# Coefficients of a state-space kernel multiplied untransposed and summed by fp32 matmuls, the table of one half built 256 channels wide, five last stores, and a new order of work

## The chip, the cores and the metric

The program runs on one core of a Trainium2 chip. The metric is the device time of one execution in microseconds, the median of several runs. A profiled execution gives a trace besides: every instruction of every engine with its start and length. TensorE (PE) does matmuls and reads its stationary operand with weight loads (PEld); VectorE (DVE), ScalarE (ACT) and GpSimd (POOL) work on tiles in on-chip memory (SBUF) and on the accumulators (PSUM); SyncE (SP) issues transfers.

## What is computed

Two branches over the same x of 2048 tokens by 512 channels are mixed by a gate per token. Branch a is a diagonal complex state-space model, applied as a causal convolution of each channel with a kernel K of 2048 taps; branch b adds a gated feed-forward result to the two tokens with the largest router value and passes the rest through.

```python
x = A_u
g = _sigmoid((x * gate_w).sum(-1, keepdims=True))
# branch a
dt = jnp.exp(log_dt)[:, None]
A = A_re + 1j * A_im
Bc = B_re + 1j * B_im
Cc = C_re + 1j * C_im
logdA = dt * A
dB = dt * Bc
P = jnp.exp(logdA[:, :, None] * l[None, None, :])
K = jnp.einsum("dn,dnl,dn->dl", Cc, P, dB).real
# y = causal convolution of u with K along the tokens, plus u * Dskip
# branch b
r = x @ w_r
idx = jnp.argsort(-r, axis=-1)[:, :C]      # C = 2
# y = (silu(x_sel @ w_gate) * (x_sel @ w_up)) @ w_down * sigmoid(r_sel), added to those two rows of x
return g * a + (1 - g) * b
```

The product C·B·dt (complex, 512 channels by 128 states) is what this text calls the coefficients. K at a tap is the sum over the states of coefficient times a power of the decay.

## The kernel before

**An order written out.** The program is a list of 651 operations, each with the buffers that it reads and writes. `ORDER` gives, as numbers in base 36, one sequence of all operations; each engine runs its own operations in that sequence, and `SECOND` says for an operation that two engines can run (an eviction by ACT or DVE, say) which of them does. Waits follow from the buffers alone: an operation waits for the last of what it needs, and for everything that used its memory before, since many buffers share places (`PLACES` gives the PSUM banks). An engine that waits holds up all that stands behind it in its own order. The operations were listed and their order was found ahead of time, with a planned cost for each.

**Stages.** (1) The parameters are loaded (`prm_l`, six tiles of 128 x 512 and log_dt), dt = exp(log_dt) is taken on ACT (`DTP`, line 589), and `DG` (line 590, DVE) holds four diagonal matrices of dt. Short matmuls with `DG` both transpose the parameters and scale them (`scaled`, line 593): the decay's real part (`AL`), its angle (`tb_`), and the two parts of B (`bd`). (2) Eight groups of transposes turn x (line 811), evicted to `XT`; reversed halves are folded (`fold`, `pm`). (3) 32 groups of four 128x512 matmuls (`forward`, line 938) transform x; their evictions fill `X`. (4) Beside that DVE and ACT build tables for each half of the channels (256 each): powers of the decay at 64 coarse taps (`tab1`, the `TP` tiles) and at fine taps (`tab2`, the `EB` and `DI` tiles, and from them, with the coefficients, the `R` tiles). (5) `kgen` multiplies the two tables on PE (line 957), which gives K at the taps needed; `kspec` transforms K (line 1009). (6) `products` multiplies the spectra on DVE (lines 1032 to 1063), `inverse` transforms back (line 1098), and each 128-token tile is scaled and stored. Routing and the feed-forward of the two tokens (lines 802 to 916) run between.

**What the change touches.** The coefficients: `ptr` (line 606) transposes C on PE into PSUM (`cc`), `scaled` transposes and scales B (`bd`), an eviction copies `cc` to SBUF (`CS`, line 633), two DVE products of 128x1024 make the four partial products (`CM1`, `CM2`, lines 634 and 635), and `WT` (lines 617 to 624, four DVE instructions of 128x256 in fp32, with a permuting read) sums them into `WW`. In `tab2` (lines 764 to 784) a loop of two passes builds the `R` tiles of a half, 128 channels each: products with `WW` (lines 772 and 773, 1024 elements), a difference and a sum (lines 774 and 775, 512 elements each), a negated copy `nb`, four products of 1792 elements (line 783) and two of 768 (line 784). `kgen` reads the tiles of pass 0 in its first eight steps and those of pass 1 in the rest (line 948). The first table load of ACT is not in the program text; it stands ahead of the first Exp. The parameter tile A_re is issued on ACT's queue, as are C_im and B_im. `warm` (line 642) are filler matmuls on PE, ten groups. The last output stores (line 1125) are eight of one tile of 128 tokens by 256 channels, four on SP and four on ACT.

Of the kernel before, what the change touches and what calls it, by code (L numbers as in the profile page):

```python
# [355 lines left out]
def small_mats():  # L356
# [15 lines left out]
    "00500200600300000101g00800400701l00u01k00900a00k00y00z01p01j01200e00d01601000b00h01300q01701801101400f00n02200c01501b02106r01m01o01d02l01z01x01c06u02f"  # L372
    "02j02n01w01v02m01y01r00j02t06s01f02h00o00i01t02g01e02u02o02k01q02r02v02i03301u02s02p02w03402a02002802306t02q02y00g02c01h00l09l03503602902705u02x02b019"
    "03705v03804l05o02605i03i09k03906v05w03j03k00w01a03l05j03a03m05k05p06w06x03n03o05s00p04m00t03p04n0b405q01n03q06y03r0b30250b205r07703z03s03t03b02d0b505m"
    "04204o03u07805t00r00m03v00v0b604r04p01i04q02z03w0790b704303x05l04004s03005n0b804100x06107a04704u04t06004v04403206205y04w04x04d05x03103c07b0b904y03f05f"
    "02404a0700720510bj04z07107c05006z05z05g04c07304b0740bi07504805206l07d04906m0530bl04e0bd07604504f05h03y07f0bb04g0540670580bk05507e07p06n0bm07h0bo056046"
    "06605907g05706904h05a0bc04i06a0ba07k0bn04j06807i06c07m07n01s07o06d0640be06b07q07j05b05c07r02e06p0bf06o05d04k07s06e05e0630bg06q00s06i07v06506j06g06f08w"
    "07t09m07l08106k09n08007y08308x0840bh08209q09o08508607z09p08707u07w07x08908a0bp08808v08b08y0bq09r06h03d0bs0br09t08d08c0bv09u08g09v08m09s08f08e08i08j09w"
    "09x08k08l0by0c00a008h08n09y0bw0a10c108o08p08q0bu08r0a20a308s09a0bt0c20c30c50a70a409z08t0bz09b08u08z0a809c09d0bx0a90aa0a509h0920ab0c40900c909e0930a609f"
    "0940c70ac0ca09i0910ad09g0950ce0cc0cb0c60al09j0cf0ci0cd0ch0c80cl0am0ck0cg0960cj0970cn0co0cm0cr0cq0cs03g0cp0cu0ct0cv0cx0an0cw0cy0d80dc0da03h0ap0980990d1"  # L380
# [19 lines left out]
def bass_gated_mix__ssm_conv_s4__moe_arch_mod__prompt_kernel(nc, A_u, A_A_re, A_A_im, A_B_re, A_B_im, A_C_re, A_C_im, A_log_dt, A_Dskip,  # L400
# [24 lines left out]
    with ExitStack() as es:  # L425
# [50 lines left out]
        def DMA(pairs, rd, wr, nbytes, eng=SP, **k):  # L476
            return P.op(eng, lambda h: [h.dma_start(o, i) for o, i in pairs], rd, wr, cost=0.5 * len(pairs), n=len(pairs), nbytes=nbytes, dma=True, **k)  # L477
# [724 lines left out]
```

## Time and profile before

| | us |
|---|---|
| median of 3 runs (lowest, highest) | 147.41 (147.23, 147.58) |
| the profiled execution | 148.09 |
| its span, first to last instruction | 146.3 |
| PE busy, DVE busy, ACT busy | 138.1, 137.3, 125.0 |
| granted PE clock | 1.000 |
| first matmul of the forward transform starts | 19.04 |
| last DVE instruction ends | 144.05 |
| issue of the last store ends | 144.42 |

Busy time is the union of an engine's instructions; consecutive instructions of DVE and ACT overlap by a little under 0.1 us, so that sums of lengths are larger than the time they take in a row. The profiled execution has 1.8 us outside its span. Where the prediction quotes a view, its columns are named there.

### The profile page before, as it was taken

To read this page: it belongs to the slowest core of one execution; us is meant where nothing else is said; L and a number is where in the kernel's file an instruction comes from. 1 tells how busy PE (TensorE), PEld (TensorE's weight loads), DVE (VectorE), ACT (ScalarE), POOL (GpSimd) and SP (SyncE) were. 2 spreads that over 40 slices of the span, in tenths; PEclk is the share of its full clock that TensorE was granted. 3 is DMA by queue.
4 is the path that set the end of the run, shared out by engine and by line. 5 is a ranking of instruction groups with operands and counts; after the bars stand their busy time and mean duration, and the time that the engine had idled before them with its cause. 6 is when DMAs were issued, how large, how long until landed. Compare 5 with 4: busy or idle time off the path is not lost.

```text
span 146.3 us, 3922 instructions
## 1 busy us (share of the span) xinstructions
PE 138.1 (94%) x1669; PEld 101.9 (70%) x1669; DVE 137.3 (94%) x195; ACT 125.0 (85%) x197; POOL 3.2 (2%) x14
## 2 busy tenths in 40 slices
PE   7967999999999999999989999989999999999992
PEld 2746855664666444697857779978774877888881
DVE  0699999999999999998999999999999999999993
ACT  4299999999999999999999897894999999796810
POOL 5001000000000000000000000100000000000000
PEclk9999999999999999999999999999999999999999
DMA  3999989401790000198000000449940001103165
GB/s 116 293 354 411 481 326 338 158 2 1 243 532 25 0 1 1 40 351 328 7 4 0 0 4 0 141 101 394 372 154 0 0 2 40 38 0 104 55 185 166
DMA packets 13610, 21.10 MB, mean 144 GB/s; under 512 B 2147, under 2 KB 9208, under 8 KB 13432
## 3 DMA queue, kind: packets, MB, share of 16 engines
q1 hardware_dynamic: 12584, 20.19, 39.3%
q10 hardware_dynamic: 1008, 0.66, 1.4%
q8 instruction: 13, 0.21, 0.6%
q14 instruction: 5, 0.04, 0.1%
HBM read 18.74 MB, written 4.20 MB: 157 GB/s over the span
## 4 chain that ended last, share of the span: by engine, by line
PE 49%; DVE 44%; ACT 2%; issue 2%; ACTq 1%; DVEq 0%
DVE AR L455 39%; PE ps L1098 17%; PE ps L938 14%; PE ps L957 3%; PE ps L1045 2%; PE ps L599 2%; DVE AR L462 2%; PE ps L647 1%; DVE AR L622 1%; PE ps L700 1%; PE ps L825 1%; PE ps L905 1%; PE ps L795 1%; ACTq L477 1%; PE ps L711 1%
## 5 line engine op out<-in xcount | busy, mean ns | idle before, releaser
L455 DVE TENSOR_TENSOR AR<-AR 128x1024 bf16<-128x1024 bf16 (+6 forms) x130 | 113.5, 933 | 3.6 <-ACT AR L466 2.8
L470 ACT ACTIVATE AR<-ps 128x1024 bf16<-128x1024 f32 (+7 forms) x63 | 51.1, 851 | 5.5 <-PE ps L1009 3.0
L466 ACT ACTIVATE AR<-ps 128x1024 bf16<-128x1024 int16 (+2 forms) x34 | 28.3, 891 | 3.6 <-PE ps L599 2.7
L938 PE MATMUL ps<-AR 128*128 128x512 bf16 x128 | 30.0, 379 | 0.0
L1098 PE MATMUL ps<-AR 128*128 128x256 bf16 x256 | 29.0, 273 | 0.0
L1098 PEld LDWEIGHTS ps<-AR 128*128 128x128 bf16 x256 | 24.9, 98 | 3.3
L938 PEld LDWEIGHTS ps<-AR 128*128 128x128 bf16 x128 | 12.1, 98 | 12.9
L1009 PE MATMUL ps<-AR 128*128 128x256 bf16 x160 | 19.1, 273 | 0.0
L957 PEld LDWEIGHTS ps<-AR 128*128 128x128 bf16 x512 | 18.1, 96 | 0.9
L957 PE MATMUL ps<-AR 128*128 128x84 bf16 (+1 forms) x512 | 18.4, 196 | 0.0
L1009 PEld LDWEIGHTS ps<-AR 128*128 128x128 bf16 x160 | 15.5, 98 | 3.1
L474 ACT ACTIVATE AR<-AR 128x256 int32<-128x256 f32 (+3 forms) x26 | 15.2, 612 | 0.1
L1107 ACT ACTIVATE AR<-ps,AR 128x256 bf16<-128x256 f32 x24 | 9.7, 479 | 2.3 <-PE ps L1098 2.2
L466 ACT ACTIVATE ps<-AR 128x256 f32<-128x256 bf16 x26 | 11.3, 488 | 0.1
L466 ACT ACTIVATE AR<-AR 128x1024 bf16<-128x1024 int16 (+4 forms) x12 | 9.4, 780 | 0.1
L647 PE MATMUL ps<-AR 128*128 128x464 bf16 x22 | 6.9, 444 | 2.0 <-DVE AR L470 1.0
L455 DVE TENSOR_TENSOR AR<-AR,ps 128x2048 bf16<-128x2048 bf16 (+1 forms) x6 | 7.1, 1210 | 0.2 <-PE ps L599 0.2
L706 PE MATMUL ps<-AR 128*128 128x512 f16 x24 | 6.2, 378 | 0.0
L1045 PE MATMUL ps<-AR 128*128 128x512 bf16 x24 | 5.8, 379 | 0.2 <-DVE AR L455 0.2
L809 PE MATMUL ps<-AR 128*128 128x128 bf16 x64 | 4.2, 219 | 1.3 <-DVE AR L455 1.3
L647 PEld LDWEIGHTS ps<-AR 128*128 128x128 bf16 x22 | 2.2, 113 | 4.2 <-issue 1.4
L809 PEld LDWEIGHTS ps<-AR 128*128 128x128 bf16 x64 | 3.7, 98 | 1.9 <-DVE AR L455 1.5
(74 smaller groups left out, 95.9 us busy)
## 6 DMA issues: line engine op xcount, KB each, us to landing
AR<-c_ksp SPq DMA_DIRECT2D x5, 512.0 KB, 7.1
AR<-in_A_u_dram SPq DMA_DIRECT2D x8, 256.0 KB, 5.3
AR<-out_dram SPq DMA_DIRECT2D x4, 512.0 KB, 9.4
AR<-c_inv SPq DMA_DIRECT2D x1, 2048.0 KB, 8.6
AR<-in_B_w_gate_dram SPq DMA_DIRECT2D x1, 1792.0 KB, 11.3
AR<-in_B_w_up_dram SPq DMA_DIRECT2D x1, 1792.0 KB, 16.8
out_dram<-AR SPq DMA_DIRECT2D x12, 128.0 KB, 2.2
AR<-c_fwd SPq DMA_DIRECT2D x4, 256.0 KB, 5.7
```

Of the source, the lines that this page charges most:

```text
L455: return P.op(DVE, lambda h: h.tensor_tensor(out=o, in0=a, in1=b, op=op), rd, wr, cost=tt_cost(o, a, b), **k)
L466: return P.op(ACT, lambda h: h.activation(out=o, in_=a, func=func, scale=scale, bias=bias), rd, wr, cost=0.185 + nel(o) * 0.833e-3 + (0.09 ...
L470: return P.op((ACT, DVE), (lambda h: h.activation(out=o, in_=a, func=ACTF.Copy), lambda h: h.tensor_copy(o, a)), rd, wr, cost=(0.185 + n * ...
L474: return P.op((ACT, DVE), (lambda h: h.activation(out=o, in_=a, func=ACTF.Copy, scale=c), lambda h: h.tensor_scalar(out=o, in0=a, scalar1= ...
L647: r = h.matmul(pb(0, 128, 0, (1, 464)), MSB(0, 128, 0, (0, 128)), MSB(0, 128, 0, (0, 464)), start=True, stop=True)
L809: last = h.transpose(bb(0, 128, db * 256 + t_ * 128, (1, 128)), U(0, 128, (2 * q + t_) * D + db * 128, (1, 128)), RV(0, 128, 0, (1, 128)) ...
L938: last = h.matmul(pb(0, 128, j * 512, (1, 512)), F[ft](0, 128, (kt * 2 + 1 - j) * 128, (1, 128)), pm[q](0, 128, kt * 512, (1, 512)), start ...
L957: last = hh.matmul(pb(0, 128, g // k * 512 + g % k * W4 + o, (1, n)), TP[h][1 - i // 2](0, 128, (b0 + g) * 128, (1, 128)), r[i](0, 128, (b ...
L1009: last = hh.matmul(pb(0, 128, n * 256, (1, 256)), KP[u](0, 128, tau * 128, (1, 128)), KC[h](0, 128, jg * 256, (1, 256)), start=(k == 0 and ...
L1045: r = hh.matmul(pb(0, 128, pm * 512, (1, W)), CB(0, 128, 128 * (k if part == 0 else 0), (1, 128)), b(0, 128, ((0, 3), (1, 2))[part][k] * 2 ...
L1098: r = hh.matmul(pb(0, 128, c0, (1, 256)), G(0, 128, ((par * 2 + part) * 4 + ft) * 512 + (2 * t2 + e) * 128, (1, 128)), X(0, 128, h * 8192 ...
L1107: return [hh.activation(out=U(0, 128, tb * D + h * HC, (1, HC)), in_=pb(0, 128, tb // 2 % 2 * 256, (1, HC)), func=ACTF.Copy, scale=SG(0, 1 ...
```

## The change

The list has 640 operations instead of 651. Its parts:

- **Coefficients.** `ptr`, the two matmul groups for B, the copy `CS`, the two products from PSUM and `WT` are gone. DVE multiplies C and B as they lie (channels not yet turned): `CM1` in one product of 1024 elements with an fp32 result, `CM2` in two of 512 (one of them negating). ACT makes an fp32 copy of dt (`DTF`) and four fp32 diagonal matrices (`DGS`) from an fp32 identity that POOL makes (`IDF`). `wsum`, two groups of eight fp32 matmuls, transposes, scales and adds in PSUM; one eviction rounds both parts into `WW` (on DVE), and `WN` is a negated copy of one part (on DVE).
- **Table.** Half 0 is built in one pass of 256 channels (`WIDE`), so `kgen(0)` reads one set of `R` tiles in all its steps; `EB`, `DI`, `NB`, `QA`, `QW` of that half move to other places. In both halves the difference and the sum become one instruction.
- **Small operations.** `LIN` lets DVE or ACT run eight operations of the routing and the gate; five of these and one copy go to ACT.
- **Stores.** The last eight stores become five: three of two tiles and two of one tile, of which only the last in the list is on ACT.
- **Head.** ACT's first instruction is an explicit table load; A_re goes to SP's queue.
- **Order.** `ORDER`, `SECOND` and `PLACES` are new throughout. Among much else: nine of the ten filler groups run ahead of the last transposes of x, the first copy of x to the output moves behind the down-projection's loads, three evictions of transposes and some scalings, negations and seeds change engine.

```diff
     def run(self, e, h):
         last = None
+        if e == ACT:
+            h.preload_act_table_set("exp_and_others")
+            last = 0
...
+WIDE = (0,)
...
+        def LIN(o, a, m, c, rd, wr):
+            one = isinstance(m, float) and m == 1.0
+            d = (lambda h: h.tensor_scalar(out=o, in0=a, scalar1=c, scalar2=None, op0=ALU.add)) if one else (lambda h: h.tensor_scalar(out=o, in0=a, scalar1=m, scalar2=c, op0=ALU.mult, op1=ALU.add)) if c is not None else (lambda h: h.tensor_scalar(out=o, in0=a, scalar1=m, scalar2=None, op0=ALU.mult))
+            f = ACTF.Copy if c is None or isinstance(c, float) else ACTF.Identity
+            P.op((DVE, ACT), (d, lambda h: h.activation(out=o, in_=a, func=f, scale=m, bias=0.0 if c is None else c)), rd, wr, cost=(0.17 + nel(o) * 0.5e-3, 0.19 + nel(o) * 0.833e-3))
...
+        CW = [HC if h_ in WIDE else QC for h_ in range(2)]
...
+        IDF = B("idf", oR + 28 * KB, 512, F32)
+        DGS = B("dgs", oR + 28 * KB + 512, 2 * KB, F32)
+        DTF = B("dtf", oR + 30 * KB + 512, 32, F32)
...
-        prm_l(0, eng=ACT)
+        diag(IDF(0, 128, 0, (1, 128)), IDF, -1, 0)
+        prm_l(0)
...
-        P.op(PE, ptr, [(PRM, 2), (PRM, 3), CBI], [cc], cost=0.45)
-        for i in range(2):
-            P.op(PE, scaled(at(bd, i * 512), 4 + i, False), [(PRM, 4 + i), DG], [(bd, i)], cost=0.225)
+        DGF = lambda k: DGS(0, 128, k * 128, (1, 128))
+        AC(DTF(0, 128, 0, (1, 4)), DTP(0, 128, 0, (1, 4)), ACTF.Copy, [DTP], [DTF])
+        for k in range(4):
+            AC(DGF(k), IDF(0, 128, 0, (1, 128)), ACTF.Copy, [IDF, DTF], [(DGS, k)], scale=DTF(0, 128, k, (1, 1)))
+        row_ = lambda i, n=1: PRM(0, 128, i * D, *(((D, n),) if n > 1 else ()), (1, D))
+        cm = lambda b, i, n=1: b(0, 128, i * D, *(((D, n),) if n > 1 else ()), (1, D))
+        TT(cm(CM1, 0, 2), row_(2, 2), PRM(0, 128, 4 * D, (0, 2), (1, D)), ALU.mult, [(PRM, 2), (PRM, 3), (PRM, 4)], [CM1])
+        TT(cm(CM2, 0), row_(2), row_(5), ALU.mult, [(PRM, 2), (PRM, 5)], [(CM2, 0)])
+        STT(cm(CM2, 1), row_(3), -1.0, row_(5), ALU.mult, ALU.mult, [(PRM, 3), (PRM, 5)], [(CM2, 1)])
+        wp = psum(2)
+        for p in range(2):
+            def wsum(hh, p=p):
+                r = None
+                for i, c in enumerate((CM1, CM2)):
+                    for k in range(4):
+                        r = hh.matmul(wp(0, 128, p * D + 4 * k, (HC, 2), (1, 4), (16, 16)), c(0, 128, (p + i) % 2 * D + k * 128, (1, 128)), DGF(k), start=i + k == 0, stop=i == 1 and k == 3, skip_group_check=True)
+                return r
+            P.op(PE, wsum, [CM1, (CM2, 1 - p), *[(DGS, k) for k in range(4)]], [(wp, p)], cost=2.2)
+        EV(WW(0, 128, 0, (1, 2 * D)), wp(0, 128, 0, (1, 2 * D)), [wp], [(WW, 0), (WW, 1)])
...
-        EV(CS(0, 128, 0, (1, 2 * D)), cc(0, 128, 0, (1, 2 * D)), [cc], [CS])
-        TT(c2(CM1), c2(CS), bd(0, 128, 0, (0, 2), (1, D)), ALU.mult, [CS, bd], [CM1])
-        TT(c2(CM2), c2(CS), bd(0, 128, D, (0, 2), (1, D)), ALU.mult, [CS, bd], [CM2])
-        WT(0, (CM1, 0), (CM2, D), ALU.subtract)
-        WT(1, (CM1, D), (CM2, 0), ALU.add)
+        SCL(WN(0, 128, 0, (1, D)), WW(0, 128, D, (1, D)), -1.0, [(WW, 1)], [WN])
...
-            for c in range(2):
-                r = RW[h][c]
+            C = CW[h]
+            for c, r in enumerate(RW[h]):
...
-                TT(w(0), w(0), q(0), SUB, [(qw, c)], [(r[0], "w")])
-                TT(w(2), w(2), q(1), ADD, [(qw, c)], [(r[2], "w")])
+                TT(pair(w(0), w(2)), pair(w(0), w(2)), pair(q(0), q(1)), ADD, [(qw, c)], [(r[0], "w"), (r[2], "w")])
...
             for b0, ng in [(8 * i, 8) for i in range(8)]:
-                r = RW[h][b0 // 32]
+                C = CW[h]
+                r = RW[h][b0 * 4 // C]
...
+                if (h, blk) == (1, 0):
+                    for t2, par, es in units:
+                        n, t0 = len(es), (2 * t2 + es[0]) * 2 + par
+                        DMA([(dr(out, token(0, 2 * t2 + es[0], par, 0) * D + h * HC, (2 * D, 128), (256 * D, n), (1, HC)), U(0, 128, t0 * D + h * HC, (2 * D, n), (1, HC)))],
+                            [x for e in es for x in uh(t0 + 2 * (e - es[0]), h)], [], 65536 * n, tag="final", eng=ACT if es == (1,) else SP)
+                    continue
```

In the new sequence the first operations of DVE are: clear, `DG`, the negated half of `CM2`, the three steps of the angle (lines 627 to 629), a scaling, `CM1`, the other half of `CM2`, a scaling, two evictions of transposes, a scaling, the angle's residual (line 632), an eviction, a scaling, an eviction, a product of 1792 elements (line 731), `WW`, an eviction, the gate weights (line 816), the folds. Those of PE are: five filler groups, `AL` first half, `tb_`, two filler groups, `AL` second half, two filler groups, two groups of transposes of x, `wsum` 0, four groups of transposes, `wsum` 1, the last two groups, the reversals, a filler group, the router's matmuls (line 825), the forward transform.

More of the change, by code (lines that the diff above doesn't have):

```diff
@@ L371 @@
 ORDER = (
[L372 to L379, printed above, removed]
@@ L616, in bass_gated_mix__ssm_conv_s4__moe_arch_mod__prompt_kernel @@
-        f512 = lambda b, c=0: b(0, 128, c, (1, D))
-        def WT(p, b0, b1, op):
-            def f(hh):
-                r = None
-                for h in range(2):
-                    n4 = lambda b, c: b(0, 128, c + 64 * h, (1, 16), (128, 4), (16, 4))
-                    r = hh.tensor_tensor(out=WW(0, 128, p * D + h * HC, (1, HC)), in0=n4(*b0), in1=n4(*b1), op=op)
-                return r
-            P.op(DVE, f, [CM1, CM2], [(WW, p)], cost=1.1)
+        DGF = lambda k: DGS(0, 128, k * 128, (1, 128))
```

107 lines of the change are left out of this document (53 added, 54 removed).

## The prediction

> **What bounds the kernel now.** First the shares of the engines and the chain that ended last (from the page), then the busy time by stage (start:end, length, each engine's busy us with its instructions).
>
> ```profile
> span 146.3 us, 3922 instructions
> PE 138.1 (94%) x1669; PEld 101.9 (70%) x1669; DVE 137.3 (94%) x195; ACT 125.0 (85%) x197; POOL 3.2 (2%) x14
> PE 49%; DVE 44%; ACT 2%; issue 2%; ACTq 1%; DVEq 0%
> ```
> ```profile
> 5.50:17.40 11.90, 9.58 (x119) 8.15 (x118) 11.28 (x20) 11.04 (x18) 0.56 (x2) 1.00 1.02 376
> 17.40:66.00 48.60, 48.17 (x552) 28.77 (x551) 48.10 (x87) 47.36 (x69) 0.00 (x0) 1.00 0.47 167
> 66.00:110.50 44.50, 43.14 (x709) 35.33 (x705) 43.84 (x46) 39.60 (x54) 0.52 (x1) 1.00 0.33 122
> 110.50:143.50 33.00, 32.91 (x284) 27.55 (x284) 32.76 (x42) 25.51 (x59) 0.00 (x0) 1.00 0.19 53
> ```
>
> Two engines bind at once. From 17.4 to 143.5 us, 126.1 us, PE is busy for 48.17 + 43.14 + 32.91 = 124.2 and DVE for 48.10 + 43.84 + 32.76 = 124.7; they idle 1.9 and 1.4 us. The end can come earlier only if both get shorter. ACT has room after 66 us, hardly before. So I keep a sum for DVE and one for PE, and the larger end decides.
>
> **The change part by part, on DVE.** The head in order of time (start, length, engine, line, what), then the groups by form (busy us, mean ns of one, idle before).
>
> ```profile
> 3.69 0.69 DVE L455 TENSOR_TENSOR AR<-AR 128x512 bf16<-128x512 bf16 x1 [2.82 <-ACT AR L466]
> 5.51 0.69 DVE L460 TENSOR_SCALAR AR<-ps 128x512 f32<-128x512 f32 x1 [1.13 <-PE ps L599]
> ...
> 7.30 0.68 DVE L470 COPY AR<-ps 128x1024 bf16<-128x1024 bf16 x1
> 7.90 0.28 DVE L474 TENSOR_SCALAR AR<-AR 128x256 int32<-128x256 f32 x1
> 8.38 2.35 DVE L455 TENSOR_TENSOR AR<-AR,ps 128x1024 f32<-128x1024 bf16 x2 [0.20 <-PE ps L599]
> ...
> 10.85 1.11 DVE L622 TENSOR_TENSOR AR<-AR 128x256 bf16<-128x256 f32 x2
> ...
> 12.49 1.09 DVE L622 TENSOR_TENSOR AR<-AR 128x256 bf16<-128x256 f32 x2
> ```
> ```profile
> L455 DVE TENSOR_TENSOR AR<-AR 128x4096 bf16<-128x4096 bf16 x14 | 31.6, 2284 | 0.0
> L455 DVE TENSOR_TENSOR AR<-AR 128x2048 bf16<-128x2048 bf16 x23 | 27.9, 1213 | 0.0
> L455 DVE TENSOR_TENSOR AR<-AR 128x1024 bf16<-128x1024 bf16 x41 | 26.6, 684 | 0.7 <-PE ps L957 0.5
> L455 DVE TENSOR_TENSOR AR<-AR 128x1792 bf16<-128x1792 bf16 x18 | 19.4, 1080 | 0.0
> L455 DVE TENSOR_TENSOR AR<-AR 128x512 bf16<-128x512 bf16 x17 | 7.0, 429 | 2.9 <-ACT AR L466 2.8
> L455 DVE TENSOR_TENSOR AR<-AR 128x768 bf16<-128x768 bf16 x8 | 4.4, 546 | 0.0
> L455 DVE TENSOR_TENSOR AR<-AR,ps 128x1024 f32<-128x1024 bf16 x2 | 2.4, 1218 | 0.2 <-PE ps L599 0.2
> ...
> L460 DVE TENSOR_SCALAR AR<-ps 128x512 f32<-128x512 f32 x1 | 0.7, 692 | 1.1 <-PE ps L599 1.1
> ...
> L474 DVE TENSOR_SCALAR AR<-AR 128x1024 bf16<-128x1024 bf16 x2 | 0.8, 406 | 0.0
> ...
> L460 DVE TENSOR_SCALAR AR<-AR 2x1 int32<-2x1 f32 x1 | 0.1, 134 | 0.0
> ```
>
> The copy at 7.30 lasts 0.68, but the next starts at 7.90: an instruction in a full queue costs its length less 0.08. All prices below are so reduced.
>
> Coefficients. Removed: the copy 0.60, two products 2.27, four sums 1.03 + 1.01; 4.91 together. Added: `CM1`, 1024 elements with an fp32 result from SBUF, a form not in the trace: between 0.60 (bf16, 684) and 1.14 (fp32 result with PSUM, 1218); I take 1.14, since the result's type is that row's. The two halves of `CM2`: 0.61 each (512 in fp32, 692). The eviction `WW`, 1024 fp32 from PSUM: the same two ends, 1.14. `WN`, 512 elements: between 0.20 (the scaling at 7.90) and 0.33 (406); 0.25. Sum 3.75; **−1.2 us**, at best −2.2.
>
> Table of half 0. Before, each pass of ten products costs 2 x 684 + 2 x 429 + 4 x 1080 + 2 x 546 = 7.64, less 10 x 0.08 = 6.84; twice, 13.7. After, nine: three of 2048 (1213), four of 3584 (2.02, between the rows of 2048 and 4096) and two of 1536 (0.95): 13.6 less 0.72 = 12.9; **−0.8**. In half 1 a pair of 429 becomes one of 684, with one overhead less, twice: **−0.2**. The negated copy of half 0 comes to DVE: **+0.3** (406 less 0.08).
>
> Moves. One eviction net to ACT −0.6; six tiny operations to ACT and one to DVE −0.25 (0.05 each, from 134); two negations to DVE +0.65; one scaling net to DVE +0.2, one of the same size to ACT −0.2. **−0.2**. ACT takes these in time that it has: its sum hardly changes. In all DVE's work shrinks by **2.1 us**.
>
> Start. DVE's second real operation is now the negated half of `CM2`, which needs C_im and B_im; queued behind it is the angle (5.51), on which all tables wait.
>
> ```profile
> 1.67 0.45 ACTq L477 DMA_DIRECT2D AR<-in_A_B_im_dram  x1
> ```
> ```profile
> AR<-in_A_B_im_dram ACTq DMA_DIRECT2D x1, 128.0 KB, 4.3
> AR<-in_A_B_re_dram SPq DMA_DIRECT2D x1, 128.0 KB, 4.0
> ```
>
> B_im, issued at 1.67, landed 4.3 later, at about 6.0. Now it is second on ACT's queue, not third (one issue of 0.45 earlier), but the table load stands ahead of both. If the queue's issues pass the table load, it lands at about 5.5; if they wait for it, some 0.8 later than before, at 6.8. The angle then starts at 6.1 to 7.4, against 5.51 with 0.61 of work not yet done: 0 to +1.3; I take 6.5, **+0.4**.
>
> The wait at `WW`. The chain of waits shows what PE's parts cost (start, length, engine, line); the groups by form show the weight loads.
>
> ```profile
> 14.81 0.45 PE ps L809 x8
> ...
> 17.60 1.58 PE ps L825 x64
> ...
> 22.70 0.22 PE ps L852 x2
> ...
> 27.04 0.39 PE ps L647 x2
> ...
> 29.82 0.39 PE ps L647 x2
> ...
> 61.81 2.19 PE ps L957 x64
> ```
> ```profile
> L852 PEld LDWEIGHTS ps<-AR 128*128 128x128 f32 x8 | 1.4, 190 | 0.5 <-DVE AR L848 0.2
> ```
>
> An fp32 matmul of 128x128 by 128 is two instructions and took 0.22 us on PE's path (line 852); eight are 1.76. But its two loads, 190 ns each, were mostly hidden under longer matmuls there; if the loads set the pace, eight cost 16 x 0.19 = 3.0. I take 1.8. With the angle at 6.5, `CM1` ends 3.0 later (0.61 + 0.35 + 0.61 + 0.20 + 1.14 in a row, with small gaps), at 9.5; `wsum` 0 ends at 11.3, four groups of transposes (0.45 each) at 13.1, `wsum` 1 at 14.9, and `WW` can start at 15.1. DVE reaches it after 5.2 us of work from 9.5, at 14.7: **+0.4**, between 0 and +2.9. Behind `WW` in DVE's queue stand an eviction, the gate weights and the folds, and PE's router matmuls and forward transform wait for those.
>
> Of the 0.6 us that DVE idled from 5.5 to 17.4 (11.90 less 11.28) I count 0.4 as replaced by these waits. DVE: −2.1 + 0.4 + 0.4 − 0.4 = **−1.7 us**.
>
> [...]
>
> **On PE.** The removed transposes and B matmuls and nine of the filler groups lie ahead of 9.5 us, where PE waits for data anyway; the sums stand in the stretch just worked out. After `wsum` 1 (14.9): two groups of transposes 0.9, two reversals 0.9, a filler 0.4: 17.2; the last eviction and the gate weights on DVE follow `WW` (15.1 + 1.14 + 0.6 + 0.1) at 17.0. So the router's matmuls start at about 17.5, as before (17.60). After them two filler groups are gone from PE's path, 2 x 0.39 = **−0.8**. Of PE's 1.9 us of idle after 17.4 some goes, as ACT and DVE run ahead; 0 to 1.9, I take 0.5. PE: **−1.3 us**, the smaller gain, and it decides.
>
> **The end.**
>
> ```profile
> 143.57 0.48 DVE L1118 TENSOR_SCALAR AR<-ps,AR 128x256 bf16<-128x256 f32 x1
> ```
> ```profile
> out_dram<-AR SPq DMA_DIRECT2D x12, 128.0 KB, 2.2
> ...
> out_dram<-AR SPq DMA_DIRECT2D x4, 64.0 KB, 1.8
> ```
>
> The last DVE operation stays the same, after the same inputs. The store of its 64 KB now stands on SP behind one of 128 KB that is issued about when it is ready, and that one lands 0.4 later after its issue: +0.1, between 0 and +0.5. The sum is −1.3 + 0.1 = −1.2: span 145.1, the profiled execution 146.9 instead of 148.09 (1.8 lie outside the span). That execution was 0.7 above the median of the runs; the median becomes 147.4 − 1.2 = **146.2**.
>
> **Rivals.** (1) The idle of both goes: PE −0.8 − 1.9 = −2.7, DVE −2.1 with nothing lost at the start less its 1.4 of idle; the smaller is −2.7, less 0.3 for what new waits remain: about 145.0. For it speaks that ACT, whose evictions PE waited for, is earlier; against it that every queue has a new sequence. (2) PE eats the gain: the router's matmuls start 1 us later, because the head waits for B_im until 6.8, and nothing of the idle goes: about 147.4. Not even that the change shortens DVE would help then. (3) Slower: the fp32 sums are paced by their loads, 3.0 each. `wsum` 0 and 1 cost 2.4 more, PE's transposes, `WW`, the folds and the forward transform all move by that: −1.2 + 2.4 = +1.2, 148.6. It decides from sums of 2.4 us each. For it speaks the 190 ns row; against it the 0.22 row, whose second instruction followed without a gap. (4) The wide table: all `R` tiles of half 0 are one set, so half 1's first write of them waits for all of `kgen(0)`, 256 matmuls, 4 x 2.19 = 8.8, with half 1's turns 10.5 us on PE, where before it waited for half of them (the idle of 0.5 by line 957 in the row of 1024). DVE has 11.2 us of other work between (16 operations that the new order puts there, at the prices above); if PE reaches `kgen(0)` more than 0.7 late, DVE waits. Late by 2.7 costs 2.0: 148.2.
>
> **How the numbers follow.** Forecast 0.42; (1) 0.15; (2) 0.15; (3) 0.14; (4) 0.14. A measurement of this kernel tells changes of about 0.2% (0.3 us) from none. Faster: 0.42 less 0.03 for its edge, and (1): 0.54. No change: (2) and 0.03, 0.18. Slower: (3) and (4), 0.28. The forecast's own range is 145.3 to 147.0, by the start (0 to +1.3), the sums and PE's idle (0 to 1.9); held to 8 in 10 over all, it goes from 144.7 to 148.5.
>
> **What would show it.** DVE busy near 135 us, `WW` a wait of half a microsecond or less, the pairs of line 852's kind in `wsum` 0.22 apart; the angle's first step at 6.1 to 7.4; the router's matmuls at 17 to 18; PE without gaps after them; the first write of half 1's `R` tiles with no idle before it. Wrong it is if `wsum` takes over 2.4 us, if the angle starts after 7.4, or if PE idles more than 2 us after 17.4.

## The result, and the profile after

The changed kernel took 146.5 us (median of 11 runs, 145.53 to 147.11), the kernel before 147.63 on the same occasions (147.23 to 148.21): so 1.1 us less by the medians. The ratio of the two is 0.9912, with a 95% interval of 0.9886 to 0.9937, which is 1.3 us less (0.9 to 1.7). The forecast was 146.2, with 1.2 us less. A few executions below took 2 to 5 us longer at a lower granted clock, the profiled one of `b_both` among them (151.93 us at 0.977), and the ratios leave them out.

The first lines of its page, with the shares of the chain that ended last:

```profile
span 144.7 us, 3933 instructions
PE 139.2 (96%) x1671; PEld 104.3 (72%) x1685; DVE 135.7 (94%) x177; ACT 125.4 (87%) x204; POOL 3.6 (2%) x16
DVE 52%; PE 35%; ACT 7%; issue 3%
```

DVE has 1.6 us less of work, in 18 instructions fewer. PE's busy time is 1.1 us longer: ahead of the router's matmuls it has 2.8 us more (16.75 against 13.95), behind them less. ACT has 0.4 us more. The head of the changed kernel in order of time:

```profile
0.75 1.28 ACT L217 ACT_TABLE_LOAD   x1 [0.75 <-PEq L1202]
...
1.20 0.46 ACTq L485 DMA_DIRECT2D AR<-in_A_B_im_dram  x1
...
4.08 0.69 DVE L465 SCALAR_TENSOR_TENSOR AR<-AR 128x512 f32<-128x512 bf16 x1 [0.34 <-DMA AR<-in_A_B_im_dram]
...
4.77 1.47 PE L613 MATMUL ps<-AR 128*128 128x128 bf16 x8
...
6.27 0.69 DVE L463 TENSOR_SCALAR AR<-ps 128x512 f32<-128x512 f32 x1 [1.50 <-PE ps L613]
...
8.40 1.82 DVE L458 TENSOR_TENSOR AR<-AR 128x1024 f32<-128x1024 bf16 x2
...
15.48 1.23 DVE L473 CAST AR<-ps 128x1024 bf16<-128x1024 f32 x1 [0.60 <-PE ps L635]
...
17.68 1.74 PE L836 MATMUL ps<-AR 128*128 128x2 bf16 x64
```

The issue of B_im went out at 1.20, in the middle of the table load (0.75 to 2.03), and its data was there at 4.08: the DMA issues on ACT's queue did not wait for the load. The angle's first step (6.27) waited 1.50 us for PE instead, whose transposes of the decay and the angle stand behind ten fillers. From the chain of waits, PE's part of the head and the end:

```profile
0.93 4.05 PE ps L659 x10
4.97 1.26 PE ps L613 x8
...
9.98 1.84 PE ps L635 x16
11.82 1.79 PE ps L820 x32
13.61 1.84 PE ps L635 x16
...
17.84 1.58 PE ps L836 x64
...
139.56 1.67 DVE AR L465 x4
141.25 0.48 DVE AR L465
141.75 0.48 DVE AR L1130
```

Each of the two sums (line 635, 16 instructions) took 1.84 us. The chain runs through PE without a gap to the router's matmuls (17.84; before 17.60), then to 109 us mostly through DVE, with ACT between 28 and 40 us, then through PE to 139.5 us, and ends on DVE.

**From the router to the end.** The run falls into two parts that behave differently. This is the stretch from the router's first matmul to the end of DVE's last operation, before and then after (start:end, length, then busy us with instructions of PE, PEld, DVE, ACT and POOL, the granted clock, DMA share, GB/s):

```profile
17.44:144.04 126.60, 124.17 (x1539) 91.65 (x1537) 125.19 (x174) 112.42 (x178) 0.52 (x1) 1.00 0.35 122
```

```profile
17.68:142.23 124.55, 122.49 (x1521) 91.28 (x1534) 123.67 (x156) 110.73 (x181) 0.52 (x1) 1.00 0.36 125
```

It is 2.05 us shorter. On DVE that is 1.52 of work and 0.53 of idle. Of PE's records 14 are missing in this trace; runs below with the same stretch have all 1535 of them, 123.47 us. So PE has 0.70 us less of work, and its idle fell from 2.43 to 1.08. ACT has 1.69 less to do there. The sum by stages: the head 0.24 later (17.68 against 17.44), this stretch 2.05 shorter, and 0.2 more from the last operation to the end of the span (144.7 − 142.23 = 2.5, before 146.3 − 144.05 = 2.25): 1.6 us, which is what the two spans show. The medians differ by less, 1.1; the next paragraphs show one thing that shifts single executions by as much.

**Half a microsecond and more that differs from run to run.** The first transposes of PE, in the kernel before and in an experiment (`b_dve`, below) that changes nothing in the head:

```profile
4.44 1.89 PE L599 MATMUL ps<-AR 128*128 128x128 bf16 x8 [0.23 <-DVE AR L455]
```

```profile
4.43 1.05 PE L599 MATMUL ps<-AR 128*128 128x128 bf16 x8 [0.31 <-DVE AR L455]
```

The same eight matmuls take 1.89 or 1.05 us. In each of the 13 traces of the table below the matmuls of the head begin at half their later pace (before: single ends 0.213 us apart, then 0.109; fillers 0.387, then 0.197), and the pace doubles at one moment, which lies between 3.9 and 6.8 us and differs from one execution to the next. The granted clock in the stages' rows is 1.00 all along and doesn't show it. The clock entries that the traces keep do: the first entry, at full speed, starts 0.1 to 0.2 us ahead of the doubling (at 6.58 before, where the pace doubles at 6.7; at 5.64 after, where it doubles at 5.8); the time ahead of it has no entry, and the rows count it as 1.00. Over the 13 traces the moment spreads over 2.9 us; what sets it, they don't show.

What it is worth is read from traces with the same head: in the kernel before, the doubling at 6.7 us puts the router at 17.44, and in `b_dve`, with its head unchanged, the doubling at 4.1 puts it at 16.73. The changed kernel's head, which its edits left alone in four experiments, has the router at 16.97 (doubling at 4.3), 17.65 (5.7), 17.82 (6.0) and 18.20 (6.8). At an equal moment the change therefore costs 0.2 to 0.8 us in the head, and with 2.05 gained behind it and 0.2 lost in the tail 1.05 to 1.65 us remain. The medians' 1.1 and the ratio's 1.3 both lie in that.

### The profile page after: what moved, and what is told of

It is laid out like the page before. It is cut to its first block, busy times and chain, and to the rows that moved or that the text cites. A ratio compares the mean times of both kernels' runs of the same rounds, so it can differ in the third digit from the quotient of the medians.

```text
span 144.7 us, 3933 instructions
## 1 busy us (share of the span) xinstructions
PE 139.2 (96%) x1671; PEld 104.3 (72%) x1685; DVE 135.7 (94%) x177; ACT 125.4 (87%) x204; POOL 3.6 (2%) x16
## 4 chain that ended last, share of the span: by engine, by line
DVE 52%; PE 35%; ACT 7%; issue 3%
DVE AR L458 47%; PE ps L1110 18%; PE ps L659 5%; ACT AR L469 3%; PE ps L635 3%; PE ps L1057 2%; PE ps L820 2%; DVE AR L465 2%; ACT AR L473 2%; ACT AR L477 2%; PE ps L613 1%; PE ps L836 1%; DVE AR L477 1%; DVE AR L859 1%; ACT AR L697 1%
## 5 line engine op out<-in xcount | busy, mean ns | idle before, releaser
L458 DVE TENSOR_TENSOR AR<-AR 128x1024 bf16<-128x1024 bf16 (+9 forms) x117 | 114.4, 1038 | 2.6 <-POOL AR L572 2.2
L473 ACT ACTIVATE AR<-ps 128x1024 bf16<-128x1024 f32 (+6 forms) x63 | 52.6, 863 | 4.8 <-PE ps L969 2.1
L949 PE MATMUL ps<-AR 128*128 128x512 bf16 x123 | 30.0, 379 | 0.3
L1110 PEld LDWEIGHTS ps<-AR 128*128 128x128 bf16 x256 | 24.9, 98 | 3.7 <-DVE AR L458 0.3
L949 PEld LDWEIGHTS ps<-AR 128*128 128x128 bf16 x128 | 12.1, 98 | 13.0
L969 PEld LDWEIGHTS ps<-AR 128*128 128x128 bf16 x512 | 18.3, 97 | 1.3 <-DVE AR L458 0.3
L1021 PEld LDWEIGHTS ps<-AR 128*128 128x128 bf16 x160 | 15.4, 98 | 3.8 <-issue 0.7
L477 ACT ACTIVATE AR<-AR 128x256 int32<-128x256 f32 (+3 forms) x22 | 12.0, 576 | 0.1
L469 ACT ACTIVATE AR<-AR 128x1024 bf16<-128x1024 int16 (+6 forms) x17 | 10.6, 645 | 1.0 <-DMA AR<-in_A_log_dt_dram 0.7
L1057 PE MATMUL ps<-AR 128*128 128x512 bf16 x23 | 5.6, 380 | 0.2
L659 PEld LDWEIGHTS ps<-AR 128*128 128x128 bf16 x22 | 2.6, 126 | 3.4 <-issue 1.9
L458 DVE TENSOR_TENSOR AR<-AR,ps 128x2048 bf16<-128x2048 bf16 x4 | 4.8, 1213 | 0.0
L477 DVE TENSOR_SCALAR AR<-AR 128x256 int32<-128x256 f32 (+3 forms) x12 | 4.1, 342 | 0.0
L723 PE MATMUL ps<-AR 128*128 128x512 bf16 x11 | 3.7, 381 | 0.4 <-issue 0.2
```

Of the source, the lines that this page charges most:

```text
L458: return P.op(DVE, lambda h: h.tensor_tensor(out=o, in0=a, in1=b, op=op), rd, wr, cost=tt_cost(o, a, b), **k)
L469: return P.op(ACT, lambda h: h.activation(out=o, in_=a, func=func, scale=scale, bias=bias), rd, wr, cost=0.185 + nel(o) * 0.833e-3 + (0.09 ...
L473: return P.op((ACT, DVE), (lambda h: h.activation(out=o, in_=a, func=ACTF.Copy), lambda h: h.tensor_copy(o, a)), rd, wr, cost=(0.185 + n * ...
L477: return P.op((ACT, DVE), (lambda h: h.activation(out=o, in_=a, func=ACTF.Copy, scale=c), lambda h: h.tensor_scalar(out=o, in0=a, scalar1= ...
L659: r = h.matmul(pb(0, 128, 0, (1, 464)), MSB(0, 128, 0, (0, 128)), MSB(0, 128, 0, (0, 464)), start=True, stop=True)
L949: last = h.matmul(pb(0, 128, j * 512, (1, 512)), F[ft](0, 128, (kt * 2 + 1 - j) * 128, (1, 128)), pm[q](0, 128, kt * 512, (1, 512)), start ...
```

## The experiments

Because of that moment the medians alone can't settle effects of half a microsecond, but the traces can: the length from the router's first matmul to DVE's last end came out as 124.55 or 124.56 in the four kernels that differ only in the head (the changed one and three experiments), whatever their heads did. The table has, for every run, the median (of 6 to 13 executions), the ratio to the kernel before on the same occasions with the 95% interval, the moment of the doubled pace (from the ends of single matmuls; a range where no matmul ran at that moment), and the two stages. The stages come from one trace of each kernel.

| run | median us | ratio | pace doubles | router at | router to DVE's end |
|---|---|---|---|---|---|
| before | 147.63 | | 6.7 | 17.44 | 126.60 |
| changed | 146.50 | 0.9912 [0.9886, 0.9937] | 5.8 | 17.68 | 124.55 |
| b_pe | 147.36 | 0.9979 [0.9959, 1.0000] | 3.9 | 16.75 | 126.14 |
| b_dve | 147.50 | 0.9994 [0.9975, 1.0012] | 4.1 | 16.73 | 126.54 |
| b_both | 147.32 | 0.9981 [0.9958, 1.0004] | | | |
| b_three | 147.45 | 0.9977 [0.9955, 0.9999] | 4.2 to 4.6 | 16.73 | 126.07 |
| a_narrow | 146.64 | 0.9923 [0.9894, 0.9952] | 6.0 | 17.82 | 125.04 |
| a_act | 146.49 | 0.9918 [0.9891, 0.9946] | 5.7 | 17.65 | 124.86 |
| a_pe | 148.06 | 1.0017 [0.9990, 1.0043] | 4.3 | 16.97 | 126.21 |
| a_dve | 146.56 | 0.9924 [0.9899, 0.9948] | 6.8 | 18.20 | 125.23 |
| a_head | 147.57 | 0.9998 [0.9985, 1.0011] | 4.2 to 4.6 | 18.40 | 124.56 |
| a_bf16 | 146.04 | 0.9896 [0.9879, 0.9914] | 4.2 | 16.55 | 124.55 |
| a_pool | 149.05 | 1.0098 [1.0083, 1.0113] | 5.3 | 17.46 | 127.11 |
| a_bf16_u | 145.78 | 0.9869 [0.9838, 0.9900] | 6.3 | 17.37 | 124.55 |

### The kernel before, made shorter on one engine, on two, on three

`b_pe`, two fillers behind the router shrunk:

```diff
-        for n in (4, 2, 2, 2, 2, 2, 2, 2, 2, 2):
+        for n in (4, 0, 2, 2, 2, 2, 0, 2, 2, 2):
...
-                for _ in range(n):
-                    r = h.matmul(pb(0, 128, 0, (1, 464)), ...
+                for _ in range(max(n, 1)):
+                    r = h.matmul(pb(0, 128, 0, (1, 464 if n else 16)), ...
```

> The kernel before, with its two pairs of filler matmuls behind the router (0.39 us each in the chain of before, 0.78 together) shrunk to one matmul of 16 columns each; nothing else. Theory on record, both engines bind (PE idles 1.9 us and DVE 1.4 us in the last 126 us): PE alone gets shorter, so the time stays, 147.6, within 0.3. Rival, PE alone binds: 0.75 less, 146.9. Rival, DVE alone binds: 147.6 as well, with PE's idle 0.7 longer.

`b_dve`, one product of the first table shrunk:

```diff
+                if (h, g) == (0, 0):
+                    TT(tr(0, 128, 0, (1, 16)), tr(0, 128, 0, (1, 16)), s(0, 128, 2 * n, (1, 16)), ALU.mult, [(s, "c")], ek)
+                    continue
                 TT(v(tr), v(tr), s(0, 128, 2 * n, (0, 2), (16, 64), (1, 16)), ALU.mult, [(s, "c")], ek)
```

> The kernel before, with one of DVE's products of 2048 elements (1.13 us on its path) cut to 16 elements, about 0.1: 1.05 us less on DVE at about 36 us; that quarter of half 0's table isn't multiplied by its cosines. Theory on record, both engines bind: the time stays, 147.6, within 0.3, since PE's work is as before. Rival, DVE alone binds: 1.05 less, 146.6. Rival, PE alone binds: 147.6.

`b_both` has both edits.

> Both edits at once, the fillers and the product: 0.78 us less on PE, 1.05 less on DVE (one product of the table is left out as in the run with that edit alone). Theory on record: the smaller of the two, 0.8 less, 146.8, and more than the sum of what the two give alone. Rival, PE alone binds: 146.9, all of it given by the fillers alone. Rival, DVE alone binds: 146.6, all of it given by the product alone.

`b_three` adds a cut on ACT:

```diff
+                    if (h, k, x) == (0, 0, "c"):
+                        l16 = bass.AP(ph.tensor, lo.offset, [lo.ap[0], [2 * HC, 4], [2, 4]])
+                        AC(s(0, 128, 2 * n, (4, 4), (1, 4)), l16, ACTF.Sin, [pb], [(s, x)], scale=SC16, tset=ts)
+                        continue
```

> The kernel before with three engines made shorter: the two filler pairs (PE, 0.78 us), the product (DVE, 1.05) and the cosines that this product reads, 16 of 1024 elements in place of all (ACT, about 0.8 less); the same quarter of half 0's table is left unmultiplied. New theory: from 17.4 to 66 us ACT binds beside PE and DVE (it idles 1.2 of 48.6 us there in the kernel before), so that PE and DVE alone gave 0.3 of 0.8; with ACT shorter too the gain is the smallest of the three, 0.8, 146.8. Rival: the rest of the 0.8 is lost after 66 us, where ACT has room; then 147.3 as without ACT's cut.

From the router to DVE's end, `b_pe`, `b_dve` and `b_three` in this order, with the columns as above:

```profile
16.75:142.89 126.14, 122.65 (x1524) 91.16 (x1535) 125.14 (x174) 112.09 (x178) 0.53 (x1) 1.00 0.36 124
```

```profile
16.73:143.27 126.54, 123.50 (x1526) 91.68 (x1537) 124.37 (x174) 112.34 (x178) 0.52 (x1) 1.00 0.36 125
```

```profile
16.73:142.80 126.07, 123.82 (x1537) 91.07 (x1535) 124.29 (x174) 111.56 (x178) 0.52 (x1) 1.00 0.35 124
```

The fillers alone gave 0.46 of their 0.78 us (126.60 to 126.14). The product, 0.82 us less of DVE's work (125.19 to 124.37), gave 0.06: it became DVE's idle. All three together gave 0.53, no more than the fillers and a little. Of `b_both` only the times are used, and they agree. So the theory on record falls in both its halves: one engine alone does shorten the run (by the trace; the interval of `b_pe`'s ratio just reaches 1.0000), and two together don't give the smaller of their gains (0.8 us expected for `b_both`, its ratio allows 0.6 at most). So does the second theory, on record with `b_three`: ACT's cut (0.86 less) added next to nothing either. At these places of the kernel before, PE's work counts for somewhat more than half, and the others' for next to nothing.

### The changed kernel, made longer on one engine

`a_narrow`, the table of half 0 in pieces of 128 channels:

```diff
+        def part(x, k):
+            return bass.AP(x.tensor, x.offset + 128 * k, list(x.ap[:-1]) + [[1, 128]])
+        def TT2(o, a, b, op, rd, wr):
+            return P.op(DVE, lambda h: [h.tensor_tensor(out=part(o, k), in0=part(a, k), in1=part(b, k), op=op) for k in range(2)][-1], rd, wr, cost=tt_cost(o, a, b))
...
+            TX = TT2 if h == 0 else TT
```

> The changed kernel, with each of the nine products of half 0's last table issued as two instructions of 128 channels: 18 instructions of 1024, 1792 and 768 elements (686, 1084, 552 ns less 0.08 each: 13.5 us) in place of nine (12.9): 0.6 us more on DVE at 52 to 67 us, nothing else. Theory, DVE's work reaches the end as long as PE has no slack to lose: 0.6 more than 146.5, 147.1. Rival, the end is PE's and DVE is ahead by 0.4 as forecast: 0.2 more, 146.7. Rival, the width matters to who waits for the tables: up to 1 us more, 147.5, with PE idle before the matmuls that use them.

`a_act`, two cosine operations in four pieces each:

```diff
+                    if h == 0 and k < 2 and x == "c":
+                        four = lambda hh, s=s: [hh.activation(out=s(0, 128, 2 * n + 4 * i, (16, 64), (1, 4)), in_=..., func=ACTF.Sin, scale=SC16, bias=0.0) for i in range(4)][-1]
+                        P.op(ACT, four, [pb], [(s, x)], cost=1.7, tset=ts)
+                        continue
```

> The changed kernel with two of ACT's cosine operations of 1024 elements issued as four of 256 each (478 ns less about 0.07 each, against 0.90): some 1.5 us more on ACT at 28 to 36 us. Theory with three binding engines: ACT idles 0.3 us from 17.4 to 66, so nearly all of it reaches the end: 1.2 to 1.5 more than 146.5, 147.8. Rival, the theory on record (PE and DVE alone bind, ACT's work is covered): 0 to 0.3 more, 146.6.

`a_pe`, two groups of forward matmuls twice:

```diff
-                            for kt in range(4):
+                            for kt in list(range(4)) * (2 if (blk, ft, q) == (0, 1, 0) else 1):
```

> The changed kernel with two groups of four forward matmuls behind the router issued twice: 1.73 us more on PE at 19 to 24 us (0.865 each). PE idles 1.84 us after 17.4. Theory that PE's work decides: 1.5 to 1.7 more, 148.1. Theory with three binding engines: some of PE's idle takes it up, most reaches the end, 1.0 to 1.7 more, 147.8. Rival, PE's fillers are cover and it has slack: under 0.6 more, 147.0.

`a_dve`, one product in 16 pieces:

```diff
+        def cut(x, i, j, m):
+            return bass.AP(x.tensor, x.offset + x.ap[1][0] * i + x.ap[2][0] * j + 64 * m, [x.ap[0], [1, 64]])
...
-                    TT(pair(p(0), p(1)), pair(Bc(eb), Bc(di)), pair(A(eb), A(eb)), MUL, ...)
+                    TT(pair(p(0), p(1)), pair(Bc(eb), Bc(di)), pair(A(eb), A(eb)), MUL, ..., cuts=h == 0)
```

> The changed kernel with one product of 1024 elements of half 0's second table issued as 16 instructions of 64 elements (by the slope between 512 and 1024 elements some 0.14 us each on the path: 2.3 in place of 0.6): 1.7 us more on DVE at about 31 us. DVE idles 0.9 us after 17.4. Theory that DVE's work decides: 1.7 more, 148.2. Theory with three binding engines: 0.8 to 1.7 more, 147.7. Rival, DVE is ahead by 0.4 and PE decides: 1.3 more, 147.8.

The same stretch of the four, `a_narrow`, `a_act`, `a_pe`, `a_dve`:

```profile
17.82:142.86 125.04, 122.82 (x1521) 91.19 (x1534) 124.19 (x165) 110.74 (x181) 0.52 (x1) 1.00 0.36 124
```

```profile
17.65:142.51 124.86, 123.80 (x1535) 91.27 (x1534) 123.75 (x156) 111.04 (x187) 0.52 (x1) 1.00 0.37 125
```

```profile
16.97:143.18 126.21, 125.13 (x1543) 92.16 (x1542) 123.77 (x156) 111.07 (x181) 0.52 (x1) 1.00 0.36 126
```

```profile
18.20:143.43 125.23, 123.93 (x1535) 91.07 (x1534) 124.50 (x171) 110.86 (x181) 0.52 (x1) 1.00 0.35 122
```

Every addition reached the end of this stretch nearly whole: the narrow table 0.52 us of DVE's work and 0.49 of time; ACT 0.31 and 0.31 (its busy time differs by 0.2 between traces with the same stretch; by the rows below it is 2 x 0.15); PE 1.66 (125.13 less 123.47) and 1.66; the cut product 0.83 and 0.68. Two doses were smaller than planned, since short instructions were cheaper than the slopes I took. The groups of the new pieces by form, `a_act` and then `a_dve`:

```profile
L735 ACT ACTIVATE AR<-ps 128x256 bf16<-128x256 int16 x8 | 2.5, 433 | 0.0
```

```profile
L461 DVE TENSOR_TENSOR AR<-AR 128x64 bf16<-128x64 bf16 x16 | 1.7, 194 | 0.0
```

Four pieces on ACT cost 1.05 us on its path in place of 0.90, and 16 on DVE about 1.6 in place of 0.6, partly beside other work. Read by the medians alone, `a_act`, `a_dve` and `a_narrow` would all have shown "no change": by their ratios they are 0.1 to 0.2 us slower than the changed kernel, each with half a microsecond either way, so that `a_dve`'s 0.68 only just lies within its interval. The lowest times (146.18 for `a_narrow`, 145.85 for `a_act`, 146.32 for `a_dve`, against 145.53) go with the stretches, but each stretch was read from one trace; only `a_pe` is clear by both. As far as that carries, PE, DVE and ACT are all tight at these places of the changed kernel: each microsecond more on any of the three cost 0.8 to 1.0. With the kernel before this gives an uneven picture: work added to the full schedule cost 0.8 to 1.0 of its length, and work taken out returned 0.46 of 0.78 us on PE and 0.06 of 0.82 on DVE.

### The head drawn together, bf16 sums, and a load moved

`a_head`: two fillers shortened, and two moves in the order (the angle's transposes ahead of the decay's, the first sums ahead of two groups of transposes):

```diff
-        for n in (4, 2, 2, 2, 2, 2, 2, 2, 2, 2):
+        for n in (4, 2, 2, 1, 2, 2, 1, 2, 2, 2):
...
-    "...00e01200f014...02n02p024...02o01d00j..."
+    "...00e01401200f...01d02n02p024...02o00j..."
```

> The changed kernel with its head drawn together on PE: two of the ten filler matmuls ahead of the first data are left out (0.39 us each), the angle's transposes come ahead of the decay's, and the first sums ahead of two groups of transposes. The angle's first step should start at 5.1 in place of 6.27, the coefficients' eviction about 1 us earlier than 15.48. Theory A, PE and DVE alone set the pace of the stretch to 50 us: 0.8 to 1.0 less than 146.5, 145.6. Theory B, ACT sets it beside them, and its first exponential (5.84) isn't earlier: 0 to 0.4 less, 146.3. The executions differ by up to 1.2 us by the moment in which PE's rate doubles (4.0 to 6.8 us in the ten traces so far), so the traces are compared from that moment on.

Its head in order of time:

```profile
5.09 0.69 DVE L463 TENSOR_SCALAR AR<-ps 128x512 f32<-128x512 f32 x1 [0.36 <-PE ps L613]
...
11.46 1.29 DVE L473 COPY AR<-ps 128x1024 bf16<-128x1024 bf16 x2 [2.23 <-PE ps L820]
...
16.20 1.23 DVE L473 CAST AR<-ps 128x1024 bf16<-128x1024 f32 x1 [0.25 <-PE ps L635]
```

The angle came at 5.09, as expected, and yet the coefficients' eviction came 0.7 us later, not 1 earlier. The first sums now stood ahead of two groups of transposes on PE; DVE's next operation was the eviction of those, and it idled 2.23 us. With a like moment of the doubled pace (`a_pe`, 4.3) the changed kernel's angle comes at 5.56, so the lead was 0.5 us, and it was lost there and more: the router started at 18.40, 1.4 later than the 16.97 of that trace. The run says nothing of my theories A and B. It shows that here the new places in the queue cost more than the 0.5 us saved in front of them.

`a_bf16`:

```diff
-        CM1 = B("cm1", oTI[1], 4 * KB, F32); CM2 = B("cm2", oTI[1] + 4 * KB, 4 * KB, F32)
+        CM1 = B("cm1", oTI[1], 2 * KB); CM2 = B("cm2", oTI[1] + 4 * KB, 2 * KB)
...
-        DGS = B("dgs", oR + 28 * KB + 512, 2 * KB, F32)
+        DGS = B("dgs", oR + 28 * KB + 512, 1 * KB)
```

> The changed kernel with CM1, CM2 and the scaled identity kept in bf16, so that the sums are bf16 matmuls: products and coefficients in a shorter type, nothing left out. CM1 686 ns in place of 1219, the halves of CM2 some 0.45 in place of 0.69: 1.0 us less on DVE; each sum 8 matmuls of 0.11, 0.9 or less in place of 1.84: 1.9 us or more less on PE. Theory A (PE and DVE set the pace to 50 us): 0.8 to 1.2 less than 146.5, 145.5. Theory B (ACT beside them): 0 to 0.4 less, 146.3.

PE's timeline shows what the shorter sums ran into:

```profile
13.84 1.36 PE L820 MATMUL ps<-AR 128*128 128x128 bf16 x16 [0.88 <-DMA AR<-in_A_u_dram]
```

The sums went from 1.84 us to 0.9, the router from 16.97 (`a_pe`, doubling at 4.3) to 16.55 (4.2): 0.4 us, at the upper end of theory B's range, but its reason (ACT) isn't what this row shows: PE waited 0.88 us for the last tile of the input. The stretch behind the router is unchanged, 124.55.

`a_bf16_u` moves one load of the forward matrices behind the last two loads of u:

```diff
-    "...02200n02l01k00k02y00m07002s02m01e00r..."
+    "...02202l01k00k02y00m07002s02m01e00n00r..."
```

> The changed kernel with the bf16 sums, and with one load of the forward matrices (256 KB, needed at 18 us) issued behind the last two loads of the input u in place of ahead of them. In the run with bf16 sums alone PE waited 0.88 us at 13.84 for the last tile of u, which landed at 13.71. Theory D, with the sums short that load sets the end of the head: u lands at about 13.0, the router's matmuls start 0.5 to 0.7 us earlier than 16.55 at the same moment of PE's doubled rate: 145.4 in place of 146.04. Rival, ACT or DVE is the next limit of the head: under 0.2 less, 145.9.

```profile
14.49 0.62 PE L820 MATMUL ps<-AR 128*128 128x128 bf16 x8 [0.49 <-ACT AR L473]
```

In PE's timeline the wait for u is gone; the same transposes now wait for evictions on ACT (0.49, and 0.30 at 15.40), as the rival had it. The pace doubled late in this execution, at 6.3, and the router came at 17.37, where the changed kernel had 17.82 at 6.0: 0.5 us or more earlier. This version has the lowest median of the study, 145.78 us, a ratio of 0.9869 to the kernel before; against the changed kernel's 0.9912 the intervals overlap, so that it is faster than that one rests on the traces. How much of it the moved load gave is not shown: no trace of `a_bf16` has so late a moment, and the medians of the two, 146.04 and 145.78, are too close.

### ACT's scalings on GpSimd

`a_pool`:

```diff
+                o_, b_ = a(0, 128, i * HC, (1, HC)), B16(0, 128, h * HC, (1, HC))
+                if pool:
+                    P.op(POOL, lambda hh, o_=o_, b_=b_, t=t: hh.tensor_scalar(out=o_, in0=b_, scalar1=float(t), scalar2=None, op0=ALU.mult), [B16], [(a, i)], cost=0.5)
+                    continue
```

> The changed kernel with the scalings of the angle by its multiples, all but the first four, on GpSimd, which has nothing else to do: 11 operations of 0.32 to 0.4 us leave ACT (4 us between 27 and 50 us), one leaves DVE. Theory B (ACT beside PE and DVE): the gain is what PE's and DVE's idle of 17 to 50 us allows, 0.3 to 0.6 less than 146.5, 146.1, with ACT idle by 3 us more. Theory C, ACT alone is the tightest and the other two follow it: 1.5 less or more, 145.0. Rival: GpSimd's operations take so long, or slow DVE's by so much, that it is slower: 147 or more.

The same stretch, and its timeline with GpSimd's operations and the wait that they caused:

```profile
17.46:144.57 127.11, 124.08 (x1535) 90.84 (x1534) 124.99 (x155) 108.14 (x170) 15.06 (x14) 1.00 0.35 123
```

```profile
25.84 4.61 POOL L691 TENSOR_SCALAR AR<-AR 128x256 int32<-128x256 f32 x4 [22.36 <-ACT AR L469]
...
37.43 2.63 POOL L691 TENSOR_SCALAR AR<-AR 128x256 int32<-128x256 f32 x3 [6.99 <-ACT AR L469]
...
40.01 0.31 POOL L681 MEMSET AR<- 128x256 bf16 x1
...
40.35 2.54 DVE L458 TENSOR_TENSOR AR<-AR 128x2048 bf16<-128x2048 bf16 x2 [1.35 <-POOL AR L681]
...
48.47 1.90 POOL L691 TENSOR_SCALAR AR<-AR 128x256 int32<-128x256 f32 x1 [7.33 <-ACT AR L473]
```

The same two products on DVE, in the changed kernel and here, where a scaling on GpSimd runs beside them:

```profile
29.08 1.28 DVE L458 TENSOR_TENSOR AR<-AR 128x1024 bf16<-128x1024 bf16 x2
```

```profile
29.05 1.48 DVE L458 TENSOR_TENSOR AR<-AR 128x1024 bf16<-128x1024 bf16 x2
```

The rival won, in both its halves. The first seven scalings take 0.85 to 1.25 us each on GpSimd (four in 4.61, three in 2.63), against 0.29 on DVE (a later one 1.90), and a clearing of 0.31 us that the changed kernel does at 15.51 now stood behind seven of them; DVE waited 1.35 us for it. And of the 20 DVE operations that ran beside a scaling nine were 0.13 to 0.20 us longer, 1.55 us together, as the second product in the rows above; the others kept their length, and what tells them apart is not shown. Behind the router the run is 2.56 us longer (127.11), of which 1.32 is DVE's longer work and 1.24 its idle, though ACT has 2.6 us less to do. With 256 elements turned into int32 the first seven scalings are three to four times as long on GpSimd as on DVE. How tight ACT alone is, this run can't tell.

## Why the prediction was right, step by step

**The total** was right, 1.1 us less against 1.2, but several of its terms were not, and they cancelled, so that its coming this close was in part luck. In the two profiled executions PE's sum is 0.24 later at the router, 0.70 less work, 1.35 less idle and 0.2 more at the end, 1.6 us less; forecast were 0, 0.8, 0.5 and 0.1.

**Start.** The angle at 6.27 lies in the range of 6.1 to 7.4, and the best guess was 6.5. The cause I named was wrong: "DVE's second real operation … needs C_im and B_im". B_im was there at 4.08, well before my 5.5 to 6.8: its issue did not wait for the table load, and it landed 2.9 us after its issue, where I had kept the 4.3 of before. What made the angle wait was PE: ten fillers up to 4.97, four transposes of the decay, then the angle's own, some of them at half pace.

**The sums and `WW`.** 1.84 us each against 1.8, `WW` at 15.48 with a wait of 0.60 against 15.1 and 0.4: right. The third rival (paced by loads, 3.0 each) is out. The loads' own row, from the groups by form, after:

```profile
L635 PEld LDWEIGHTS ps<-AR 128*128 128x128 f32 x32 | 3.7, 192 | 0.0
```

A load lasts 192 ns, and yet 16 matmuls passed in 1.84 us, one every 0.115: the loads overlap one another, each starting 0.112 us after the last. It is twice as long as the bf16 loads of line 820 (98 ns on average); that it would set the pace, as the rival had it, is not so.

**DVE's work.** I had 2.1 us less; the page has 1.6. The rows that I could price came out as priced:

```profile
L458 DVE TENSOR_TENSOR AR<-AR 128x1024 f32<-128x1024 bf16 x1 | 1.2, 1219 | 0.0
L458 DVE TENSOR_TENSOR AR<-AR 128x3584 bf16<-128x3584 bf16 x4 | 7.9, 2002 | 0.0
L458 DVE TENSOR_TENSOR AR<-AR 128x1536 bf16<-128x1536 bf16 x2 | 1.9, 946 | 0.0
```

`CM1` 1219 ns, the products of 3584 elements 2.00 us, those of 1536 0.95. The missing 0.5 lies in the tables together (DVE's products behind the head shrank by 0.7 us, moved ones left out, in place of 1.0) and in small terms. The width of the table is worth 0.49 us of time by `a_narrow`.

**The router and the head.** "The router's matmuls start at about 17.5, as before" failed: 0.24 later in the two profiled executions, and 0.2 to 0.8 at an equal moment of PE's doubled pace, which I had no trace to see from. It also lay in the base: the profiled execution of before, 0.7 above the median of its first runs, had its pace doubled at 6.7, among the latest of the traces.

**PE after the router.** "Two filler groups are gone from PE's path": PE's work is 0.70 less, for 0.78. But "0 to 1.9, I take 0.5" for its idle was the term that was mis-sized: its idle fell by 1.35. Where, the list of waits tells, before and then after (us in total, times, longest):

```profile
PE ps L969 <- ACT AR L470: 1.0, 2, 0.7
...
PEld ps L905 <- DVE AR L455: 0.7, 1, 0.7
PEld ps L892 <- ACT AR L474: 0.7, 1, 0.7
```

```profile
PEld ps L981 <- ACT AR L473: 0.6, 1, 0.6
...
PEld ps L923 <- ACT AR L477: 0.4, 1, 0.4
```

The selections of both halves (line 969 before, 981 after) waited for ACT's evictions, the feed-forward's matmuls (892, 905) for ACT and DVE. PE's own waits there add up to 1.6 us before. After, no matmul behind the router waits 0.2 us or more for another engine; only weight loads still do, among them those of one selection (0.6 in place of 1.8) and of the feed-forward's transposes (923, 0.4 as before), where PE itself idles 0.1 us and not at all. ACT reaches the router with 1.7 us less left to do, DVE with 1.5. This is a good part of the first rival ("the idle of both goes"): 1.35 of PE's idle, 0.53 of DVE's.

**What bounds.** "The end can come earlier only if both get shorter" is not how this kernel behaved: PE alone gave 0.46 of 0.78, DVE 0.06 of 0.82. And I left out ACT ("takes these in time that it has"), where 0.31 us more cost 0.31.

**The other rivals.** (2) was near in the head, by another cause, and was outweighed; its time was also added up too low, for a router 1 us later, fillers of 0.8 less and the 0.1 of the tail make 0.3 more, 147.7, not 147.4. (4) didn't come. From the trace, the last of the 256 matmuls of `kgen(0)` ended at 72.39, and half 1's first write of an `R` tile started at 72.67; this piece of the chain of waits, in which it lies, runs through DVE alone:

```profile
71.52 3.90 DVE AR L458 x6
```

The margin was 0.28 us, where I had 0.7. **The tail** cost 0.2 in place of 0.1.

**What stays open.** Of the 2.05 us behind the router the wide table explains 0.49 and the fillers 0.46, the one measured by taking it out of the changed kernel, the other by shrinking them in the kernel before. The remaining 1.1 us, with ACT's earlier start and the new order in it, was not separated: the order comes as one piece. Nor was the change's head tried with another place of the decay's transposes alone.

## What to carry to other kernels

Where three engines are full at once, price a change by stages: here a stretch of the trace between two fixed events repeated to 10 ns (124.55 or 124.56 us in four kernels) while the whole time of one kernel scattered by 1.6 us (145.53 to 147.11), so that edits of 0.3 us are read there and not from medians. In this case an edit that took work off one of several full engines returned 0.46 of 0.78 us or 0.06 of 0.82, and one that added work cost nearly all of it (0.68 of 0.83 up to 1.66 of 1.66); so count what the other queues wait for, and not the idle of one engine. And a step that is moved ahead in one queue delays what it passed (in `a_head` DVE then idled 2.23 us): look up who waits for that first.

## What the runs showed of the hardware that was not expected

- The matmuls' pace doubled at 3.9 to 6.8 us in the 13 traces, at a moment that differs from one execution to the next, with a granted clock of 1.00 in the rows of the stages; it is worth up to 0.7 us of the time before and 1.2 of the changed kernel.
- DMA issues on ACT's queue went out at 0.78 and 1.20 while ACT loaded its table (0.75 to 2.03).
- The fp32 weight loads of 192 ns overlapped one another: they start 0.112 us apart, 16 with their matmuls in 1.84 us.
- Short instructions were cheap: a product of 64 elements took 0.10 us on DVE's path (`a_dve`), 256 elements 0.26 on ACT's (`a_act`); GpSimd took 0.85 to 1.90 us for 256 elements in the rows of `a_pool`.
- Nine of 20 DVE operations beside GpSimd's scalings were 0.13 to 0.20 us longer, as in a pair of products of 1024 elements that took 1.48 in place of 1.28.
